# A later date for the first head's maxima, and half-tiles for the last four units' copies, in a fused attention and gated-MLP kernel

## The chip, the cores and the metric

The kernel runs on one core of one Trainium2 chip. The metric is the device time of one execution in microseconds (us). Before the change the median of three runs is 2565.24 us (2562.74 to 2565.86).

## The reference, cut to what matters

```python
def _A_ref(x, wqkv, wo):                      # 32 heads of 18
    q, k, v = split_heads(x @ wqkv)
    scores = jnp.einsum("bhqd,bhkd->bhqk", q, k) * (Dh ** -0.5)
    p = _softmax(scores, axis=-1)
    o = jnp.einsum("bhqk,bhkd->bhqd", p, v)
    return merge_heads(o) @ wo

def _B_ref(x, w_gate, w_up, w_down):
    g = jnp.einsum("bsd,df->bsf", x, w_gate)
    u = jnp.einsum("bsd,df->bsf", x, w_up)
    return jnp.einsum("bsf,fd->bsd", g * u, w_down)

xn = _layernorm(x)                            # x: 1 x 2048 x 576, F = 4608
out = x + _A_ref(xn, wqkv, wo) * _silu(_B_ref(xn, w_gate, w_up, w_down))
```

## The kernel before

Every product is made of float32r pieces: an operand is split into a high part and the rest, and three products of parts stand for one. The kernel has three stages: q, k and v from the normalised x (to about 190 us), a long middle (to about 2497 us), and the output products with `wo` (to the end).

**The middle.** TensorE is used as two halves of 64 rows, and two streams of matmuls run beside each other, stream 0 on rows 0 to 63 and stream 1 on rows 64 to 127. The gated MLP is cut into 72 units `u` = (chunk of 512 tokens, 256 columns of F). For a unit the streams make the up and gate products of its two blocks `n` = 2u and 2u+1 (27 matmuls of 512 columns for each block and stream, line 703), and after the gate and up products of the unit that follows they make the down products of unit `u` (48 matmuls of 288 columns for each stream, line 749). When the two of a block are done, VectorE multiplies them (line 715), ScalarE takes the high part into `hs[u]` (line 719), and GpSimd the rest (line 720). The down products of a half need the other half's rows too, so `turn_round` (line 726 and after) copies `hs[u]` with the halves exchanged into `hx[u]` by DMA. There is one buffer `hx`. For most units the copy is one pair of DMAs of 512 KB each, issued when the down products of the unit before are through (line 787). The last two units are copied in two parts, each as soon as its block of `hs` is there; of these, the first goes to a tile `hxl` in the buffer `acc` of the first accumulators, which are no longer used then.

**Attention** runs between these matmuls. Head by head, 64 products `a` (line 624) give scores whose row maxima VectorE takes (line 626); `max_rows` turns the 2048 maxima round and writes them into `pair`, rows 64 and after, with four DMAs from GpSimd's queue (line 646). Then 64 products `b` (line 656) give the transposed scores with the maximum subtracted, in two PSUM banks in turn, and ScalarE takes the exponential (line 658). The probabilities times v (line 667) take the whole array, in visits in which neither stream runs; the last visit of a head comes after its last exponential. After a head's last visit VectorE normalises (lines 679 to 684) and four DMAs store the result in `sot`; for the last head these are on SyncE's queue.

**The order** is not found on the chip: a planner (`order`, with `can_go`, `visit`, `b_ready` and their tables) runs while the program is built. It keeps a clock for each stream, free times for VectorE, ScalarE and GpSimd, and one clock for transfers (`moved`). From these it picks the next matmul. Every engine then works through its own list in that order and waits at semaphores. `rows_done[h]` is the planner's date for the maxima of head `h` in `pair`: the end of the last reduction plus `ROWS` = 6.0 us. `there["h", u]` is its date for the copy of `hs[u]`; a stream whose next matmul needs it later than its clock is held, and the other goes on alone. What the planner doesn't know is the time that an engine's queue needs to issue DMAs. After the last gate product `wo_load` (line 820 and after) loads `wo` with six DMAs from ScalarE's queue.

**After the middle** SyncE's queue loads the attention output back (`fetch_o`, lines 843 and 846), the silu of the MLP (line 871) and x (line 873), in the order of the code. ScalarE and VectorE split what came (lines 851 and 856), and 28 matmuls for each of 16 row tiles (line 1295) make the output.

Of the kernel before, what the change touches and what calls it, by code (L numbers as in the profile page):

```python
# [40 lines left out]
def kernel(  # L41
# [115 lines left out]
    units = [(c, q) for c in range(NCH) for q in range(NF2)]  # L157
# [160 lines left out]
    FIRST = (0, 1)  # L318
# [265 lines left out]
    n = 8  # L584
# [21 lines left out]
    with ExitStack() as mid:  # L606
# [103 lines left out]
        def gate_end(n, ps):  # L710
            u, j = divmod(n, 2)
            if j == 0:
                hs[u] = gp.tile([128, 2, 2, 512], FR, name="hs", bufs=2)
            h32 = us.pop(n)
            nc.vector.tensor_tensor(h32, ps, h32, op=OP.mult)  # L715
            if g_after(n):
                g_get(g_after(n))
            hj = hs[u][:, j]
            nc.scalar.activation(hj[:, 0, :], h32, AF.Copy)  # L719
            nc.gpsimd.tensor_tensor(hj[:, 1, :], h32, hj[:, 0, :].bitcast(FT), op=OP.subtract)  # L720
            if u == 0 or u >= len(units) - 2:
                turn_round(u, j)

        hx = {}

        def turn_round(u, j):

            if u >= len(units) - 2:
                if j == 0 and u == len(units) - 2:
                    hx[u] = accp.tile([128, 2, 2, 512], FR, name="hxl", tag="acc")  # L730
                elif j == 0:
                    hx[u] = gp.tile([128, 2, 2, 512], FR, name="hx", bufs=1)
                js = slice(j, j + 1)
            else:
                if u or j == 0:
                    hx[u] = gp.tile([128, 2, 2, 512], FR, name="hx", bufs=1)
                js = slice(0, 2) if u else slice(j, j + 1)
            for r in range(2):
                nc.sync.dma_start(hx[u][half[r], js].bitcast(FT), hs[u][half[1 - r], js].bitcast(FT))
# [28 lines left out]
        def down_end(r, u, s, ps):  # L768
            c, q = units[u]
            cs = slice(r * HALF, (r + 1) * HALF)  # L770
            if q == 0 and c >= 2:
                ready(sdone, 4 * c - 8 + s)
            a = sums(4 * c + s)[:, cs]
            if q == 0:
                nc.vector.tensor_copy(a, ps[:, 0:HALF])  # L775
            else:
                nc.vector.tensor_tensor(a, a, ps[:, 0:HALF], op=OP.add)  # L777
            if q == NF2 - 1 and c < NCH - 1:
                seen[c, s] = seen.get((c, s), 0) + 1
                if seen[c, s] == 2:  # L780
                    silu_store(4 * c + s)
            if s == 3:
                seen[u] = seen.get(u, 0) + 1
                if seen[u] == 2:
                    d_get(u + 1)
                    if u + 1 < len(units) - 2:
                        turn_round(u + 1, 1)

        def silu(t, new, end):
# [140 lines left out]
        TOTAL = H * N  # L930
        LEAD, MOST = 24, 40
        EARLY, LOAD, BEHIND = 0.17, 0.10, 10.0
        PACE, SKEW, PULL, FIRST, ROWS = 1.005, 3.0, 3.0, 2.0, 6.0
        slots, gone = [0, 0], [0.0, 0.0]
        clk, free = [0.0, 0.0], {"DVE": 0.0, "ACT": 0.0, "POOL": 0.0}
        TAIL = {"DVE": 0.095, "ACT": 0.115, "POOL": 0.04}
# [67 lines left out]
        def a_next(r=0):  # L1004
            nonlocal na
            h, i = divmod(na, N)
            feed(0, h, i)
            a_item(h, i, r)
            slot = turn["a"] % 2
            turn["a"] += 1  # L1010
            banks["a"][slot] = engine("DVE", issue(r, LONG), 0.60) + EARLY
            na += 1
            if i == N - 1:
                max_fold(h)
                max_rows(h)
                rows_done[h] = engine("DVE", 0.0, 0.85) + ROWS

        def b_ready(r=1):
            h = nb // N
# [137 lines left out]
        def order():  # L1157
# [6 lines left out]
            while any(heads) or na < TOTAL or nb < TOTAL or due:  # L1164
# [34 lines left out]
                if can and (at <= clk[r] + 0.01 and (goal <= clk[r] or blocked) or op is None and (at <= clk[r] or not held)):  # L1199
                    clk[r] = max(clk[r], at)  # L1200
                    score(r)
                elif op is not None:
                    length, first, work, end, (kind, n, k) = op
                    if first:
                        clk[r] = max(clk[r], next_free("g"))
                        slots[r] = banks["g"].index(next_free("g"))
                        banks["g"][slots[r]] = 1e9
                    work()
                    lands = issue(r, length)
                    gone[r] += length  # L1210
                    if end:
                        done = engine(end[0], lands, end[1])
                        banks["g"][slots[r]] = done + EARLY
                        if kind == "d":
                            if k == 47:
                                parts.setdefault(n, []).append(clk[r])
                                if len(parts[n]) == 2:
                                    downed[n] = moved(max(parts[n]) + 0.3, 1.18) if (n + 1) % NF2 and n + 2 < len(units) else 0.0
                                    if n + 3 < len(units):
                                        there["h", n + 1] = moved(max(parts[n]) + 1.0, 1.05)  # L1220
                        elif r == 0:
                            upped[n] = done
                        else:
                            gated[n] = done
                            fin = engine("ACT", done + 0.05, 0.535)
                            fin = engine("POOL", fin + 0.05, 1.29)
                            if n != 2:
                                anew = 4 * NF2 - UNSAVED <= g_after(n) < 4 * NF2
                                loaded[g_after(n) - 2] = moved(done - 0.4, 1.18) if (n // 2 + 1) % NF2 and not anew else 0.0
                            if n // 2 >= len(units) - 2:  # L1230
                                there["h", n // 2] = moved(fin, 0.524) - (0.0 if n // 2 < len(units) - 1 else 1.1)
                            elif n < 2:
                                there["h", 0] = moved(fin, 0.524)
                            for _ in range(2):
                                hot = n + 2 >= 2 * NF2 and n % (2 * NF2) in (34, 35, 0) and n + 2 < 2 * len(units)
                                for want in stacks:
                                    if hot and (want[0] is load_pair or n % (2 * NF2) == 2 * NF2 - 1):
                                        continue
                                    stacks.remove(want)
                                    send(want, fin + 1.4)  # L1240
                                    break
                    heads[r] = next(feeds[r], None)
                else:
                    clk[r] = max(clk[r] + 0.05, min(clk[1 - r] + 0.01, clk[r] + 0.3))
# [120 lines left out]
```

## Time and profile before

| | |
|---|---|
| median of three runs | 2565.24 us (2562.74 to 2565.86) |
| the profiled execution's own time | 2566.68 us |
| its span, first to last instruction | 2564.9 us |
| TensorE busy | 2544.2 us, 99% |
| VectorE, ScalarE, GpSimd busy | 75%, 57%, 24% |
| mean granted TensorE clock | 0.999 |
| chain that ended last | TensorE 95%, DMA 2%, VectorE 2% |

An engine's busy time is the union of its instructions; TensorE counts as busy when one of its two halves works, so 99% does not say that both do. A row of idle time names the instruction or transfer that ended it. Times in the rows are microseconds from the span's start.

### The profile page before, as it was taken

The page shows a single profiled execution, that of the slowest core. Times are in us where ns is not written, and L with a number is a line of the kernel's source. Part 1 is how long each engine was busy: PE and PEld are TensorE (multiplying, and loading weights), DVE is VectorE, ACT ScalarE, POOL GpSimd, SP SyncE. Part 2 cuts the span into 40 slices and gives each one's busy share as a digit, 9 for nine tenths or more (in the row PEclk, how much of TensorE's full clock was granted, in tenths as well). Part 3 has the DMA queues.
Part 4 walks back from the last instruction along what each step waited for, and adds up shares of the span by engine and source line. Part 5 has one row for each costly group of instructions (what it writes and reads, how often), then busy time and mean ns, then how long its engine had stood idle before and what let it go on. Part 6 is the DMA issues. An engine that isn't in the chain of part 4 may idle for free.

```text
span 2564.9 us, 59227 instructions
## 1 busy us (share of the span) xinstructions
PE 2544.2 (99%) x24360; PEld 2115.4 (82%) x24360; DVE 1933.2 (75%) x3377; ACT 1473.1 (57%) x2712; POOL 618.9 (24%) x687
## 2 busy tenths in 40 slices
PE   8999999999999999999999999999999999999998
PEld 7899888787888888878888888778888888888878
DVE  6208678877778888777878888777889887778537
ACT  5222666666666655556666665555656656556651
POOL 3214334443421111112311111111111121111125
PEclk9999999999999999999999999999999999999999
DMA  7796889889775656576766566565666666664567
GB/s 246 234 293 163 222 220 244 222 217 248 199 222 173 183 174 185 173 183 186 214 201 174 172 178 184 168 178 154 180 204 164 175 190 176 178 175 142 160 194 248
DMA packets 203979, 499.87 MB, mean 195 GB/s; under 512 B 57744, under 2 KB 125200, under 8 KB 165948
## 3 DMA queue, kind: packets, MB, share of 16 engines
q1 hardware_dynamic: 193020, 482.86, 66.7%
q0 software_dynamic: 9952, 11.74, 1.7%
q8 instruction: 192, 3.15, 0.5%
q10 hardware_dynamic: 736, 1.47, 0.2%
q14 instruction: 79, 0.65, 0.1%
HBM read 307.49 MB, written 107.61 MB: 162 GB/s over the span
## 4 chain that ended last, share of the span: by engine, by line
PE 95%; DMA 2%; DVE 2%; ACT 0%; SPq 0%; POOL 0%; issue 0%; ACTq 0%; DVEq 0%
PE pg L703 35%; PE pg L667 17%; PE pg L749 15%; PE pa L624 11%; PE pb L656 9%; PE pg L423 2%; PE pa L368 2%; PE pb L368 2%; PE pg L1295 1%; DVE mx L626 0%; DMA sqk<-hl 0%; PE pa L1295 0%; PE pb L1295 0%; DMA hx<-hs 0%; DMA xi<-in_A_x_dram 0%; DMA gin<-sg 0%
## 5 line engine op out<-in xcount | busy, mean ns | idle before, releaser
L626 DVE TENSOR_REDUCE mx<-pa 128x1 f32<-128x512 f32 x2048 | 1364.7, 686 | 222.7 <-PE pa L624 114.1
L658 ACT ACTIVATE pt<-pb 128x512 f32<-128x512 f32 x2048 | 1160.8, 598 | 532.9 <-PE pb L656 477.2
L703 PE MATMUL pg<-xc,wgu 64*128 64x512 f32 x7722 | 1358.1, 388 | 0.0
L703 PEld LDWEIGHTS pg<-xc,wgu 64*128 64x128 f32 x7722 | 1048.2, 184 | 36.0 <-DVE acc L775 0.2
L656 PE MATMUL pb<-pair,ring 64*128 64x512 f32 x2016 | 784.6, 395 | 2.6 <-DMA pair<-mt 2.6
L624 PE MATMUL pa<-pair,ring 64*128 64x512 f32 x2008 | 778.2, 393 | 1.1 <-DVE mx L626 1.1
L749 PE MATMUL pg<-wd,hs 64*128 64x288 f32 x3408 | 582.2, 292 | 0.3 <-DVE acc L777 0.2
L749 PE MATMUL pg<-wd,hx 64*128 64x288 f32 x3360 | 567.7, 292 | 0.0
L749 PEld LDWEIGHTS pg<-wd,hs 64*128 64x128 f32 x3408 | 489.0, 185 | 5.5 <-issue 0.8
L720 POOL TENSOR_TENSOR hs<-us,hs 128x512 fp32r<-128x512 f32 x144 | 186.3, 1293 | 1262.6 <-ACT hs L719 1251.5
L749 PEld LDWEIGHTS pg<-wd,hx 64*128 64x128 f32 x3360 | 477.9, 185 | 3.0
L667 PE MATMUL pg<-pt,vt 128*32 128x512 f32 x4096 | 454.8, 594 | 1.0 <-DVE acc L777 0.9
L624 PEld LDWEIGHTS pa<-pair,ring 64*128 64x128 f32 x2008 | 364.9, 184 | 68.3 <-issue 51.1
L656 PEld LDWEIGHTS pb<-pair,ring 64*128 64x128 f32 x2016 | 366.0, 184 | 9.5 <-issue 2.9
L667 PEld LDWEIGHTS pg<-pt,vt 128*32 128x32 f32 x4096 | 125.5, 110 | 284.7 <-issue 278.3
L777 DVE TENSOR_TENSOR acc<-acc,pg 128x288 f32<-128x288 f32 x544 | 231.6, 443 | 26.4 <-PE pg L749 22.7
L673 DVE TENSOR_TENSOR oc<-oc,pg 128x512 f32<-128x512 f32 x69 | 47.2, 685 | 217.3 <-PE pg L667 217.2
L719 ACT ACTIVATE hs<-us 128x512 fp32r<-128x512 f32 x144 | 91.0, 632 | 140.2 <-DVE us L715 139.2
L206 POOL TENSOR_TENSOR wgu<-wraw,wgu 128x384 fp32r<-128x384 f32 x129 | 129.5, 1020 | 98.3 <-ACT wgu L205 81.5
L671 ACT ACTIVATE oc<-pg 128x512 f32<-128x512 f32 x32 | 19.1, 598 | 188.3 <-PE pg L667 181.8
L646 POOL DMA_DIRECT2D pair<-mt x128 | 77.9, 614 | 178.5 <-DVE mt L641 171.9
L715 DVE TENSOR_TENSOR us<-pg,us 128x512 f32<-128x512 f32 x144 | 98.5, 684 | 26.3 <-PE pg L703 18.0
(147 smaller groups left out, 1394.4 us busy)
## 6 DMA issues: line engine op xcount, KB each, us to landing
wgu<-swg SPq DMA_DIRECT2D x94, 1152.0 KB
hx<-hs SPq DMA_DIRECT2D x138, 512.0 KB
wd<-swd SPq DMA_DIRECT2D x50, 1152.0 KB
swg<-wgu SPq DMA_DIRECT2D x36, 1152.0 KB
pair<-sqk SPq DMA_DIRECT2D x192, 144.0 KB
ring<-sqk SPq DMA_DIRECT2D x384, 72.0 KB
swd<-wd SPq DMA_DIRECT2D x18, 1152.0 KB
sqk<-hl SPq DMA_DIRECT2D x32, 512.0 KB
```

What stands on the lines that cost most here:

```text
L206: nc.gpsimd.tensor_tensor(w[:, 9 + b:12 + b, :], raw[:, b:b + 3, :], w[:, b:b + 3, :].bitcast(FT), op=OP.subtract)
L368: nc.tensor.matmul(p, wq[b, a], xcs[c][:, e, :], start=n == 0, stop=n == len(PAIRS) - 1)
L624: nc.tensor.matmul(p, q[rows, t * 128:(t + 1) * 128], k[rows, c * 512:(c + 1) * 512], start=True, stop=True)
L626: nc.vector.tensor_reduce(mx[h][:, t, c:c + 1], p, axis=AX.X, op=OP.max)
L656: nc.tensor.matmul(p, k[rows, t * 128:(t + 1) * 128], q[rows, c * 512:(c + 1) * 512], start=True, stop=True)
L658: nc.scalar.activation(pt[t, c], p, AF.Exp, scale=scale)
L667: nc.tensor.matmul(p[32 * c:32 * c + 32, :], vt[h // 2][:, t, 6 * (h % 2):6 * (h % 2) + 32], pt[t, c], start=t == ts[0], stop=t == ts[-1])
L703: nc.tensor.matmul(ps, gw[n][half[r], a, :], xg[i][half[r], e, :], start=k == 0, stop=k == len(TERMS) - 1)
L715: nc.vector.tensor_tensor(h32, ps, h32, op=OP.mult)
L720: nc.gpsimd.tensor_tensor(hj[:, 1, :], h32, hj[:, 0, :].bitcast(FT), op=OP.subtract)
L749: nc.tensor.matmul(ps[:, 0:HALF], (hx if k else hs)[u][half[r], j, a, s * 128:(s + 1) * 128], dw[u][half[r], k, j, e, :], start=n == 0, st ...
L777: nc.vector.tensor_tensor(a, a, ps[:, 0:HALF], op=OP.add)
```

## The change

Two things are changed. `CROWDED` = 9.0 takes the place of `ROWS` = 6.0 in the planner's date for the maxima of head 0. And the rule for the last two units (copy `hs` in two parts, each when its block is ready) now holds for the last four, 68 to 71; the even ones of them, 68 and 70, go into the buffer `acc`, the odd ones into `hx`. The planner's dates follow.

```diff
-            if u == 0 or u >= len(units) - 2:
+            if u == 0 or u >= APART:
                 turn_round(u, j)
 
         hx = {}
+        APART = len(units) - 4
 
         def turn_round(u, j):
 
-            if u >= len(units) - 2:
-                if j == 0 and u == len(units) - 2:
+            if u >= APART:
+                if j == 0 and u % 2 == 0:
                     hx[u] = accp.tile([128, 2, 2, 512], FR, name="hxl", tag="acc")
...
-                    if u + 1 < len(units) - 2:
+                    if u + 1 < APART:
                         turn_round(u + 1, 1)
...
-        PACE, SKEW, PULL, FIRST, ROWS = 1.005, 3.0, 3.0, 2.0, 6.0
+        PACE, SKEW, PULL, FIRST, ROWS, CROWDED = 1.005, 3.0, 3.0, 2.0, 6.0, 9.0
...
-                rows_done[h] = engine("DVE", 0.0, 0.85) + ROWS
+                rows_done[h] = engine("DVE", 0.0, 0.85) + (ROWS if h else CROWDED)
...
-                                    if n + 3 < len(units):
+                                    if n + 1 < APART:
                                         there["h", n + 1] = moved(max(parts[n]) + 1.0, 1.05)
...
-                            if n // 2 >= len(units) - 2:
+                            if n // 2 >= APART:
                                 there["h", n // 2] = moved(fin, 0.524) - (0.0 if n // 2 < len(units) - 1 else 1.1)
```

Most of the program stands as it did. On TensorE's list two stretches differ: 255 matmuls from the first `b` on, and 681 matmuls in the last 100 us of the middle. Lines after 722 are one higher in the changed kernel.

TensorE, where the products `b` of the first head begin (pb are their banks, line 656; pa are products `a` of the second head; pg with xc and wgu are up and gate products). Before:

```order
L749 MATMUL pg<-wd,hx 128x288
L656 MATMUL pb<-pair_1152,ring 128x512
L703 MATMUL pg<-xc,wgu 128x512
L656 MATMUL pb<-pair_1152,ring 128x512
L703 MATMUL pg<-xc,wgu 128x512 x2
L624 MATMUL pa<-pair_1153,ring 128x512
L703 MATMUL pg<-xc,wgu 128x512 x2
L624 MATMUL pa<-pair_1153,ring 128x512
L703 MATMUL pg<-xc,wgu 128x512 x9
```

In the changed kernel, the last rows ahead of its first `b` and those up to shortly after the second:

```order
L703 MATMUL pg<-xc,wgu 128x512 x15
L624 MATMUL pa<-pair_1153,ring 128x512
L703 MATMUL pg<-xc,wgu 128x512 x13
L624 MATMUL pa<-pair_1153,ring 128x512
L703 MATMUL pg<-xc,wgu 128x512 x4
L656 MATMUL pb<-pair_1152,ring 128x512
L703 MATMUL pg<-xc,wgu 128x512 x3
L656 MATMUL pb<-pair_1152,ring 128x512
L624 MATMUL pa<-pair_1153,ring 128x512
L703 MATMUL pg<-xc,wgu 128x512
L624 MATMUL pa<-pair_1153,ring 128x512
L703 MATMUL pg<-xc,wgu 128x512
```

Between the last down product and the first `b` there are now 57 matmuls of 512 columns, where there was none.

SyncE, from the copy for unit 67 on (hx and hxl from hs are the copies, wgu and wd the weights' loads, ring a load for attention). Before:

```order
L739 DMA hx<-hs 64x2048 x2
L197 DMA wgu<-swg 128x2304 x2
L265 DMA ring<-sqk 18x1024 x3
L240 DMA wd<-swd 128x2304
L739 DMA hx<-hs 64x2048 x2
L197 DMA wgu<-swg 128x2304 x2
L265 DMA ring<-sqk 18x1024 x3
L240 DMA wd<-swd 128x2304
L739 DMA hx<-hs 64x2048 x2
```

In the changed kernel:

```order
L740 DMA hx<-hs 64x2048 x2
L197 DMA wgu<-swg 128x2304
L740 DMA hxl<-hs 64x1024 x2
L197 DMA wgu<-swg 128x2304
L740 DMA hxl<-hs 64x1024 x2
L265 DMA ring<-sqk 18x1024 x3
L240 DMA wd<-swd 128x2304
L197 DMA wgu<-swg 128x2304
L740 DMA hx<-hs 64x1024 x2
L197 DMA wgu<-swg 128x2304
L740 DMA hx<-hs 64x1024 x2
L240 DMA wd<-swd 128x2304
```

The copies for units 68 and 69 now stand ahead of the load of `wd` that they stood behind.

ScalarE, at the end of the middle (pt from pb are the exponentials, us the end of an up product, hs the high part of a block of the last unit, wor the six loads of `wo`, and the names in brackets are the semaphores waited for, DMAHW those of transfers, of which there are eight). Before:

```order
L658 ACTIVATE pt<-pb 128x512 [waits PE_49] x6
L708 ACTIVATE us<-pg 128x512 [waits PE_49,Pool_49]
L658 ACTIVATE pt<-pb 128x512 [waits PE_49]
L719 ACTIVATE hs<-us 128x512 [waits DVE_49]
L825 DMA wor<-in_A_wo_dram 128x576 [waits DMAHW0_49,PE_49]
L825 DMA wor<-in_A_wo_dram 128x576 [waits DMAHW2_49]
L825 DMA wor<-in_A_wo_dram 128x576 [waits DMAHW3_49]
L825 DMA wor<-in_A_wo_dram 128x576 [waits DMAHW5_49]
L827 DMA wor<-in_A_wo_dram 64x576 [waits DMAHW6_49]
L827 DMA wor<-in_A_wo_dram 64x576 [waits DMAHW7_49]
L863 ACTIVATE wos<-wor 128x576 [waits DMAHW0_49,PE_49]
```

In the changed kernel:

```order
L708 ACTIVATE us<-pg 128x512 [waits PE_49,Pool_49]
L658 ACTIVATE pt<-pb 128x512 [waits PE_49] x3
L719 ACTIVATE hs<-us 128x512 [waits DVE_49]
L826 DMA wor<-in_A_wo_dram 128x576 [waits DMAHW3_49]
L826 DMA wor<-in_A_wo_dram 128x576 [waits DMAHW5_49]
L826 DMA wor<-in_A_wo_dram 128x576 [waits DMAHW6_49]
L826 DMA wor<-in_A_wo_dram 128x576 [waits DMAHW0_49]
L828 DMA wor<-in_A_wo_dram 64x576 [waits DMAHW1_49]
L828 DMA wor<-in_A_wo_dram 64x576 [waits DMAHW3_49]
L658 ACTIVATE pt<-pb 128x512 [waits PE_49] x13
L864 ACTIVATE wos<-wor 128x576
```

The last thirteen exponentials, which stood ahead of the loads of `wo`, now stand behind them, and the sixth load waits for the semaphore of the first.

## Rows read from the trace of the kernel before

**Rows 1.** The page, busy time of each engine (us, share of the span, instructions).
```profile
PE 2544.2 (99%) x24360; PEld 2115.4 (82%) x24360; DVE 1933.2 (75%) x3377; ACT 1473.1 (57%) x2712; POOL 618.9 (24%) x687
```

**Rows 2.** What TensorE's matmuls waited for: total us, times, longest.
```profile
PE pb L656 <- DMA pair<-mt: 2.6, 1, 2.6
```

**Rows 3.** Timeline at the first head: start, us, instruction [idle before it <- releaser].
```profile
255.98 1.28 ACT L658 ACT_TABLE_LOAD   x1
...
257.81 0.46 PE L656 MATMUL pb<-pair,ring 64*128 64x512 f32 x1 [2.63 <-DMA pair<-mt]
...
258.31 1.08 ACT L658 ACTIVATE pt<-pb 128x512 f32<-128x512 f32 x2 [1.05 <-PE pb L656]
```

**Rows 4.** TensorE by the microsecond: us, busy (matmuls), granted clock, DMA share, GB/s.
```profile
258.00:259.00 1.00, 1.00 (x9) 0.80 1.02 277
259.00:260.00 1.00, 1.00 (x8) 0.50 1.25 234
260.00:261.00 1.00, 1.00 (x8) 0.50 1.25 249
261.00:262.00 1.00, 1.00 (x7) 0.50 1.08 229
262.00:263.00 1.00, 1.00 (x12) 0.99 0.94 205
```

**Rows 5.** All matmuls in three stretches of the last 100 us of the middle.
```profile
2410.00:2415.00 5.00, 5.00 (x47) 1.00 1.00 135
2435.00:2440.00 5.00, 5.00 (x48) 1.00 1.03 295
2440.00:2445.00 5.00, 5.00 (x37) 1.00 0.98 289
```

**Rows 6.** Down products (line 749) alone, in two of these; weight loads stand second.
```profile
2410.00:2415.00 5.00, 1.90 (x12) 1.65 (x12) 1.00 1.00 135
...
2440.00:2445.00 5.00, 1.09 (x7) 1.04 (x8) 1.00 0.98 289
```

**Rows 7.** ScalarE's timeline where the middle ends (ACTq: issued by its queue).
```profile
2479.07 0.60 ACT L658 ACTIVATE pt<-pb 128x512 f32<-128x512 f32 x1
2480.48 0.63 ACT L719 ACTIVATE hs<-us 128x512 fp32r<-128x512 f32 x1 [0.81 <-DVE us L715]
2480.55 2.40 ACTq L825 DMA_DIRECT2D wor<-in_A_wo_dram  x4
2482.99 1.42 ACTq L827 DMA_DIRECT2D wor<-in_A_wo_dram  x2
2484.51 0.69 ACT L863 ACTIVATE wos<-wor 128x576 fp32r<-128x576 f32 x1 [3.40 <-DMA wor<-in_A_wo_dram]
...
2495.40 0.63 ACT L851 ACTIVATE hi<-o 128x512 fp32r<-128x512 f32 x1 [9.11 <-DMA o<-sot]
```

**Rows 8.** The last two loads of `wo`: duration ns min/median/max, first and last start.
```profile
L827 ACTq DMA_DIRECT2D wor<-in_A_wo_dram x2: 535/692/849, 2483.0 to 2483.6; - x2
```

**Rows 9.** TensorE's timeline: last visit, and the output products' begin and pause.
```profile
2480.90 3.64 PE L667 MATMUL pg<-pt,vt 128*32 128x512 f32 x32
...
2497.32 2.04 PE L1295 MATMUL pa<-wos,hi 128*128 128x288 f32 x12 [0.52 <-DVE acc L777]
...
2513.86 1.03 PE L1295 MATMUL pa<-wos,hi 128*128 128x288 f32 x6 [1.22 <-DVE ys L1304]
```

**Rows 10.** VectorE's timeline: the last head's first and last step after its last visit.
```profile
2484.69 0.69 DVE L673 TENSOR_TENSOR oc<-oc,pg 128x512 f32<-128x512 f32 x1 [3.88 <-PE pg L667]
...
2487.07 0.71 DVE L684 STREAM_TRANSPOSE oc<-tp 128x512 f32<-128x512 f32 x1
```

**Rows 11.** SyncE's queue after it: stores of the last head, reloads of heads.
```profile
2487.81 2.94 SPq L687 DMA_DIRECT2D sot<-oc  x4
2491.41 3.62 SPq L843 DMA_DIRECT2D o<-sot  x5
```

**Rows 12.** What SyncE's queue waited for, 2470 to 2520 us.
```profile
SPq L843 <- DMA hx<-hs: 0.5, 1, 0.5
```

## The prediction

> **What bounds the kernel now.** I read the page first: TensorE is busy 99% of the span, every other engine 75% or less [rows 1]. So only three things can move the time: TensorE waiting, TensorE at its lower clock, or one of its two halves working alone, which the busy time does not show. The list of what matmuls waited for has one DMA in it, once, for 2.6 us [rows 2]; the timeline puts it at 257.81 us, before the first product `b` of the first head, which waits for its maxima in `pair` [rows 3]. The windows by the microsecond show what came of it: once TensorE ran again, its granted clock was 0.80, 0.50, 0.50 and 0.50 of full speed for four microseconds, that is 1.2 instead of 2.4 GHz, and then full again [rows 4]. The third thing shows in the number of matmuls: 48 long ones in 5 us where both streams run, 47 and 37 in two stretches of the last 100 us, of which 12 and 7 are short [rows 5, 6]. Last I read the end of the middle engine by engine, because the output products there begin when a chain over four engines is through [rows 7 to 11].
>
> **The first head.** The maxima come when they come: four DMAs behind the second head's work, landed at 257.81. What the change moves is the matmuls. 57 long ones now stand before the first `b`. At 0.11 us each (5 us for 48, of which some four are cut by the stretch's edges) they take 6.4 us, so that `b` is reached at about 255.2 + 6.4 = 261.6, some 4 us after the landing. These 57 are up and gate products of unit 3 and products `a`; in the kernel before they followed directly on the first `b` without any wait of their own, so their operands were there by 258, and most were before. Removed: the wait, 2.63 us, and the lower clock, 0.20 + 0.50 + 0.50 + 0.50 + 0.01 = 1.71 us of full-speed work [rows 3, 4]. Sum 4.3 us.
>
> Added: ScalarE loads the table of the exponential just ahead of its first one. In the kernel before these 1.28 us lay inside the wait [rows 3]. Now an up product's end (its copy, 0.60 us) stands ahead of the load, and the third `b`, which needs the first one's bank, stands 18 matmuls (2.3 us, some of them alone in their half) behind the last matmul of that up product. The copy starts 0.45 us after that matmul (from `b` at 257.81 to its exponential at 258.31 it is 0.50 [rows 3]); then 0.60 + 1.28 + 0.60 follow, together 2.9 us. The third `b` waits 0.6 to 0.7 us. Bounds 0 (the load gets in before the copy) and 1.4 (load and gate's split both ahead). I take 0.7: the first head gives **3.6 us back** (2.9 to 4.3). A short wait like this I count without a clock penalty.
>
> The Trainium skill, "ScalarE: Activation LUTs", section "Table sets: the hidden batching unit", puts a table load at about 2.7 us. The trace has 1.28 [rows 3]. By the page another 1.4 us would be lost here, and the sum below would come to 2572.5 us.
>
> **The copies.** Those of units 68 and 69 leave earlier, and the planner no longer holds a stream for them. In the kernel before, 2440 to 2445 has 30 long and 7 short matmuls; a short one is 288/512 of a long one, so that is 34 of 48, and 2410 to 2415 is 35 + 6.7 = 42 of 48. The 14 and 6 that are missing, at 0.11 us, make 1.5 + 0.7 = **2.2 us** by which the last gate product comes earlier. The copies in parts cost SyncE four more issues; on that queue nothing near is late for it. The waits that the parts add are for buffers used two units before, long free; the first accumulators are through since chunk 2. I cost both at nothing; if a copy were late the down products behind it would wait, at up to 2 us.
>
> **What that sets free, and what is late next.** The planner now puts thirteen products `b` of the last head after the last gate product, where there were none. Their exponentials stand on ScalarE's queue behind the six loads of `wo`. The split that precedes the loads began at 2480.48 [rows 7]; 2.2 us earlier is 2478.3. The loads held the queue from 2480.55 to 2484.41, 3.86 us, and nothing else stood behind them but the split of `wo` itself. In the changed program the sixth also waits for the semaphore of the first, which had landed by 2484.51, 3.96 us after its issue [rows 7]; with 0.54 to 0.85 us for the sixth's own issue [rows 8] the queue is held 4.5 to 4.8 us. I take 4.7 (bounds 3.9 and 4.8). ScalarE is free at 2483.0.
>
> Thirteen exponentials at 0.60 us [rows 7] follow. The banks are two, so the last `b` goes in after the eleventh exponential, at 2489.6, and the last visit, 32 matmul rows in 3.64 us [rows 9], runs from 2489.9 to 2493.5. It had run from 2480.90 to 2484.54. So the last visit ends **9.0 us later**. TensorE is in order: the last unit's down products stand behind that visit, and the third of the thirteen `b` makes TensorE wait from about 2479.2 to 2483.6.
>
> Behind the visit comes the chain that I take as fixed: VectorE from 2484.69 to 2487.78, stores of the last head on SyncE's queue until 2490.75 [rows 10, 11], then the reloads of heads, which are behind these stores on the same queue though most of them don't need them. Of the 0.66 us to 2491.41, 0.5 was a wait for a copy of the last unit [rows 12] that will be long done. So the reloads are 8.5 us later, and with them ScalarE's split of the first (2495.40 [rows 7]) and the first output product (2497.32 [rows 9]): 2505.8.
>
> Two clock losses lie on this. The wait of 4.4 us is longer than the one of 2.63 us after which the clock fell [rows 3, 4]; but after it the exponentials set the pace, which hides most of the 1.7 us. I take 0.5 (0 to 1.7). Before the output products TensorE will have been idle from about 2500.5 to 2506, far longer than 2.63 us, and works at once at its own limit: 1.7 us more, as in rows 4 (0 to 3.4). Against that, the pause of 1.2 us at 2513.86 [rows 9] is taken up by TensorE being late anyway. The tail: 8.5 + 0.5 + 1.7 - 1.2 = **9.5 us more** (7 to 12).
>
> **The sum.** 9.5 - 3.6 = 5.9 us more. The profiled execution took 2566.68 us with a span of 2564.9, so it would take 2572.6; it lay 1.4 us above the median of the runs, so the median would go from 2565.24 to **2571.1 us**, +0.23%. The likeliest case's own range, from the bounds, is 2567.5 to 2574.5. A measurement of this kernel can tell about 0.2% (5.1 us) from no change, so the forecast stands near that line.
>
> **Rivals.** *The loads don't hold ScalarE* (not slower). The queue goes on to the exponentials while transfers are being set up. They would start at 2478.9, the eleventh ends at 2485.5, and the visit at 2489.4, 4.9 us late; reloads 4.4 late, clock and pause as above: tail +4.9, sum +1.3, 2566.5 us. It decides whether the first exponential behind the loads starts within a microsecond of the split. Against it: the split of `wo` began 0.1 us after the last issue, though that fits a wait for its data too [rows 7]. Chance 0.12. The Trainium skill, "DMA: Bandwidth & Descriptors", section "Anatomy of one DMA — SWDGE (gpsimd) path", gives about 50 ns for a sequencer's dispatch of a DMA, there on GpSimd's path. By that rule six would hold a queue for 0.3 us, and this rival would be the result; the trace has 3.86 us for six [rows 7].
>
> *The same mechanism, smaller*: the queue is held 3.9 us, the clock does not fall at the wait, the idle time before the output products costs less than 1 us. Tail 9.5 - 0.8 - 0.5 - 1.0 = 7.2, or less where the first head gives 4.3: sum +2.9, 2568.1 us, within 0.2%. Chance 0.30.
>
> *The first head's wait is exchanged, not removed*: the third and later `b`, held at the table load, or VectorE behind the products `a` that come sooner, stop TensorE for long enough that the clock falls again. Then only some 1 us is won there, and the sum is +8.5, 2573.7 us. For it speaks that the second head's `a` and the first `b` now lie closer; against it that VectorE idled right after the stall. Chance 0.10.
>
> *The tail is not late at all* (the planner's order holds on the chip, both gains arrive): -3.6 - 2.2 = -5.8, 2559.4 us. It would need exponentials that are not held, and stores that don't keep back the reloads. Chance 0.04.
>
> **How the numbers follow.** The forecast has the remaining 0.44. Slower by over 0.2%: 0.44 + 0.10 = 0.54. Within 0.2%: 0.30 + 0.12 = 0.42. Faster: 0.04. The range 2564.5 to 2575.5 takes in the first three rivals and the bounds, and leaves out the last one and the far ends of both sides.
>
> **What would show it.** Right: no matmul waits for `pair`, and no half clock near 260 us; an idle time of about 0.7 us before the third `b`; in the tail, the six loads on ScalarE's queue followed by thirteen exponentials in a row, TensorE waiting 3 to 5 us for the first of them, the last visit ending some 6 us later than before (9.0 less the first head's gain), the first output product some 5 us later, with a lower clock around it. Wrong: exponentials that run between the loads' issues; a matmul that waits for `hx` or `hxl`; or a new wait of microseconds between 258 and 270.

## The result, and the profile after

Over 19 runs each, the kernel before has a median of 2564.37 us (2561.18 to 2568.22) and the changed one of 2569.02 us (2564.31 to 2570.76): ratio 1.0018, 95% interval [1.0012, 1.0024]. It is 4.65 us slower, just inside the 0.2% within which the prediction calls a time the same; 5.9 us were forecast. The changed kernel's profiled execution took 2569.04 us, at its median, with a span of 2567.3 us. That of before lay 2.3 us above the median of its 19 runs, so the two spans differ by 2.4 us only. What follows counts between these two traces, and in medians where runs are compared.

The list of what TensorE's matmuls waited for, after (total us, times, longest), has no `pair` any more, and a new first entry from the middle:

```profile
PE pb L656 <- ACT pt L658: 4.5, 3, 3.8
```

**The first head**, timeline and TensorE's windows by the microsecond (us, busy, matmuls, granted clock, DMA share, GB/s), answering to [rows 3, 4]:

```profile
260.63 0.60 ACT L708 ACTIVATE us<-pg 128x512 f32<-128x512 f32 x1 [4.86 <-PE pg L703]
...
260.91 0.39 PE L656 MATMUL pb<-pair,ring 64*128 64x512 f32 x1
...
261.25 1.28 ACT L658 ACT_TABLE_LOAD   x1
...
263.20 0.49 PE L656 MATMUL pb<-pair,ring 64*128 64x512 f32 x1 [0.39 <-ACT pt L658]
```

```profile
260.00:261.00 1.00, 1.00 (x12) 1.00 0.94 213
261.00:262.00 1.00, 1.00 (x10) 1.00 1.14 229
262.00:263.00 1.00, 0.80 (x4) 1.00 0.96 221
```

The first `b` runs at 260.91 without a wait, the clock stays full, and what is left is 0.39 us before the third `b`, behind the copy of the up product and the table load.

**The end of the middle**, ScalarE (ACTq: issued by its queue), answering to [rows 7]:

```profile
2472.30 0.63 ACT L719 ACTIVATE hs<-us 128x512 fp32r<-128x512 f32 x1
2472.31 2.85 ACTq L826 DMA_DIRECT2D wor<-in_A_wo_dram  x4
2475.20 1.76 ACTq L828 DMA_DIRECT2D wor<-in_A_wo_dram  x2
2477.01 1.09 ACT L658 ACTIVATE pt<-pb 128x512 f32<-128x512 f32 x2 [4.07 <-DMA wor<-in_A_wo_dram]
...
2485.56 1.78 ACT L658 ACTIVATE pt<-pb 128x512 f32<-128x512 f32 x3 [0.16 <-PE pb L656]
```

The six loads hold the queue from 2472.31 to 2476.96, 4.65 us; the thirteen exponentials follow. TensorE, answering to [rows 9]:

```profile
2477.66 0.79 PE L656 MATMUL pb<-ring,pair 64*128 64x512 f32 x1 [3.82 <-ACT pt L658]
...
2486.64 3.64 PE L667 MATMUL pg<-pt,vt 128*32 128x512 f32 x32
...
2497.46 0.37 PE L1296 MATMUL pa<-wos,hi 128*128 128x288 f32 x1 [0.64 <-DVE acc L778]
2499.06 0.40 PE L1296 MATMUL pa<-wos,hi 128*128 128x288 f32 x1 [1.24 <-ACT hi L852]
2500.16 3.02 PE L1296 MATMUL pa<-wos,hi 128*128 128x288 f32 x10 [0.70 <-ACT hi L852]
```

TensorE waits 3.82 us for the first of these exponentials. The last visit ends at 2490.28 where it had ended at 2484.54. The first output product comes about when it did before, but the row of ten starts 2.8 us later than the first row of before, and slowly. The clock, in windows of 5 us:

```profile
2475.00:2480.00 5.00, 2.34 (x18) 0.62 1.02 276
2480.00:2485.00 5.00, 5.00 (x53) 0.70 0.40 85
...
2495.00:2500.00 5.00, 2.59 (x30) 1.00 0.78 220
2500.00:2505.00 5.00, 4.84 (x24) 0.66 1.01 316
```

It is at its lower level for some microseconds after both waits. Behind the visit, VectorE's first step and SyncE's queue (SPq), answering to [rows 10, 11]:

```profile
2490.42 0.69 DVE L673 TENSOR_TENSOR oc<-oc,pg 128x512 f32<-128x512 f32 x1 [4.23 <-PE pg L667]
```

```profile
2493.41 1.38 SPq L687 DMA_DIRECT2D sot<-oc  x4
2495.01 2.28 SPq L844 DMA_DIRECT2D o<-sot  x5
```

The starts of the same place in TensorE's list, us, put the pieces in order:

```
number of the matmul in the list       before     after   difference
1600   (ahead of the first head)       253.03    252.26    -0.77
2000   (behind it)                     298.63    294.06    -4.57
22960  (ahead of the last 100 us)     2402.35   2398.10    -4.25
24000  (among the output products)    2509.28   2513.30    +4.02
24359  (the last)                     2558.36   2560.92    +2.56
```

The first head gave 3.8 us and the end of the middle took 8.3. Among the output products, where the pause of 1.22 us in [rows 9] is gone, 1.46 came back. Between the two places where the order differs nothing of note happened.

### The profile page after: what moved, and what is told of

It reads as the page before. It is cut to its first block, busy times and chain, and to the rows that moved or that the text cites. A ratio compares the mean times of both kernels' runs of the same rounds, so it can differ in the third digit from the quotient of the medians.

```text
span 2567.3 us, 59234 instructions
## 1 busy us (share of the span) xinstructions
PE 2544.7 (99%) x24360; PEld 2114.7 (82%) x24360; DVE 1930.3 (75%) x3377; ACT 1472.1 (57%) x2712; POOL 617.3 (24%) x687
## 4 chain that ended last, share of the span: by engine, by line
PE 98%; DVE 1%; DMA 0%; ACT 0%; issue 0%; SPq 0%; ACTq 0%; DVEq 0%
PE pg L703 35%; PE pg L667 18%; PE pg L750 16%; PE pa L624 11%; PE pb L656 9%; PE pg L423 2%; PE pa L368 2%; PE pb L368 2%; PE pg L1296 1%; PE pa L1296 1%; DVE mx L626 1%; PE pb L1296 1%; DVE us L715 0%; DMA xin<-in_A_x_dram 0%; DMA wor<-in_A_wo_dram 0%; PE pg L354 0%
## 5 line engine op out<-in xcount | busy, mean ns | idle before, releaser
L750 PE MATMUL pg<-wd,hx 64*128 64x288 f32 x3312 | 559.6, 292 | 0.0
L750 PEld LDWEIGHTS pg<-wd,hx 64*128 64x128 f32 x3312 | 470.8, 185 | 2.8
```

What stands on the lines that cost most here:

```text
L750: nc.tensor.matmul(ps[:, 0:HALF], (hx if k else hs)[u][half[r], j, a, s * 128:(s + 1) * 128], dw[u][half[r], k, j, e, :], start=n == 0, st ...
```

## The experiments

All are timed against the kernel before, run beside them; the short diffs are against the changed kernel unless they say otherwise.

**One part at a time.**

```diff
-        APART = len(units) - 4
+        APART = len(units) - 2
```

> Only the later date for the first head's maxima; the copies in parts stay with the last two units. Theory (the two parts are independent; the loss is in the tail): the first head gives back 3.8 us, as in the changed kernel, and the tail is that of the kernel before: 2564.4 - 3.8 = 2560.6 us, ratio 0.9985. Rival (the wait is only passed on and comes back in the 2000 us that follow): within 1 us of the kernel before, ratio 0.9996 to 1.0004.

Measured: 2561.22 us against 2564.30, ratio 0.9989 [0.998, 0.9998]. 3.1 us faster, so the gain of the first head does not come back later, and this kernel beats both.

```diff
-                rows_done[h] = engine("DVE", 0.0, 0.85) + (ROWS if h else CROWDED)
+                rows_done[h] = engine("DVE", 0.0, 0.85) + ROWS
```

> Only the copies in parts for the last four units; the first head as before. Theory: the whole loss is here, 2569.0 + 3.8 = 2572.8 us, ratio 1.0033; the trace shows the wait for the maxima of 2.6 us and, in the last 100 us, the same wait of TensorE of about 3.8 us for an exponential behind the loads of wo. Rival (the loss comes from both changes together): below 2569, ratio under 1.0018.

Measured: 2571.81 us, ratio 1.0029 [1.0019, 1.004]: 7.5 us slower. Its list of waits has both:

```profile
PE pb L656 <- ACT pt L658: 3.9, 2, 3.7
PE pb L656 <- DMA pair<-mt: 2.4, 1, 2.4
```

7.5 - 3.1 = 4.4 us against the 4.65 of both together: the parts add up, and the whole loss lies in the copies' part. This trace holds a surprise too. TensorE waits 2.43 us at the first head, and the clock does not fall after it:

```profile
257.00:258.00 1.00, 0.29 (x2) 1.00 0.22 61
258.00:259.00 1.00, 1.00 (x12) 1.00 0.88 229
```

**What holds ScalarE.**

```diff
-                nc.scalar.dma_start(wov["raw"][:, k, :], wo[128 * k:128 * k + 128, :])
+                nc.sync.dma_start(wov["raw"][:, k, :], wo[128 * k:128 * k + 128, :])
...
-                nc.scalar.dma_start(wov["raw"][b:b + 64, 4, :], wo[512:576, :])
+                nc.sync.dma_start(wov["raw"][b:b + 64, 4, :], wo[512:576, :])
```

> The changed kernel with the six loads of wo on SyncE's queue, behind the copies for the last unit, so that nothing holds ScalarE between the last split and the thirteen exponentials; TensorE's order is the same to the row. Theory (the issue of six loads on ScalarE's queue is the cause): the wait of 3.8 us before the third of the thirteen products goes, and with it the half clock behind it; the last visit starts some 6 us earlier than 2486.6, the output products follow it, and a pause of 1.2 to 1.5 us returns among them: 2569.0 - 6.3 + 1.4 = 2564 us (2561 to 2566), ratio about 1.000. Rival (thirteen exponentials after the last gate product are too late by themselves, with two banks): the last visit moves by less than 2 us, 2567.5 us or more, ratio 1.0012 or more.

Measured: 2562.97 us, ratio 0.9994 [0.9985, 1.0003]; 6.05 us less than the changed kernel's median. ScalarE and the last visit in its trace:

```profile
2472.99 0.63 ACT L719 ACTIVATE hs<-us 128x512 fp32r<-128x512 f32 x1
2473.53 2.30 ACT L658 ACTIVATE pt<-pb 128x512 f32<-128x512 f32 x4
```

```profile
2480.86 3.64 PE L667 MATMUL pg<-pt,vt 128*32 128x512 f32 x32
```

TensorE's order is the same to the row. The exponentials now follow the split at once, and the visit starts 5.8 us earlier. The granted clock stays at 1.00 from 2470 to 2512 us, so the 6.05 us are those of the wait, of the late visit and of both stretches at the lower clock together. So the queue that issues the loads of `wo` was the cause. Of the pause that was expected back among the output products only 0.3 us came.

The control is the kernel before with the same edit:

> The kernel before with the six loads of wo on SyncE's queue: the control to the changed kernel with the same edit. Theory (the hold of ScalarE costs only where something that TensorE needs stands behind the loads, and before the change only the split of wo did): no change, ratio 0.9995 to 1.0005, where the same edit took 6 us from the changed kernel. Rival (the loads on ScalarE's queue cost time in both kernels): 3 us or more faster, ratio 0.9988 or less.

Measured: 2563.67 us against 2564.78, ratio 1.0000 [0.9991, 1.0009]. Where only the split of `wo` stands behind the loads, what the hold costs lies within some 2 us of nothing; the same edit took 6.05 us from the changed kernel.

The dose, twelve loads of half the rows on ScalarE's queue:

```diff
-                nc.scalar.dma_start(wov["raw"][:, k, :], wo[128 * k:128 * k + 128, :])
+                for p in (0, 64):
+                    nc.scalar.dma_start(wov["raw"][p:p + 64, k, :], wo[128 * k + p:128 * k + p + 64, :])
...
-                nc.scalar.dma_start(wov["raw"][b:b + 64, 4, :], wo[512:576, :])
+                for p in (0, 32):
+                    nc.scalar.dma_start(wov["raw"][b + p:b + p + 32, 4, :], wo[512 + p:544 + p, :])
```

> The changed kernel with the six loads of wo cut into twelve of half the rows, on the same queue of ScalarE: the same bytes, twice the issues. Theory (the number of issues sets how long ScalarE is held): it is held for some 8 to 9 us instead of 4.65, TensorE waits about 4 us longer, 2573 us, ratio 1.0034. Rival (what holds ScalarE is the bytes or the time to the landing): no change, 2569 us, ratio 1.0018.

Measured: 2574.11 us, ratio 1.0041 [1.0028, 1.0053], 5.1 us more than the changed kernel. Its queue and its wait:

```profile
2472.61 7.05 ACTq L827 DMA_DIRECT2D wor<-in_A_wo_dram  x8
2479.70 2.81 ACTq L830 DMA_DIRECT2D wor<-in_A_wo_dram  x4
```

```profile
2483.20 0.79 PE L656 MATMUL pb<-ring,pair 64*128 64x512 f32 x1 [9.06 <-ACT pt L658]
```

The same bytes in twice the issues hold the queue for 9.9 us instead of 4.65, so neither the bytes nor one landing sets the hold; it grows with the number of issues. The average of 0.8 us for each is made of unequal pieces, though. The six of the changed kernel (duration in ns, smallest, median and largest, then first and last start):

```profile
L826 ACTq DMA_DIRECT2D wor<-in_A_wo_dram x4: 389/444/1449, 2472.3 to 2473.7; - x4
L828 ACTq DMA_DIRECT2D wor<-in_A_wo_dram x2: 472/500/529, 2475.2 to 2476.5; - x2
```

The sixth load begins 1.3 us after the fifth, which took about 0.5: the 0.8 us between are its wait for the landing of the first, whose semaphore it uses again. With twelve, the last four wait likewise for about 1.1 of their 2.8 us.

**The wait, or the late visit?** TensorE's wait of 3.82 us looks like the loss itself. To tell it from the late visit, the planner is told of the hold, so that it puts other work into it:

```diff
                                     moved(max(clk), 1.47)
+                                    engine("ACT", max(clk), 4.5)
```

> The changed kernel; its planner books 4.5 us of ScalarE at the loads of wo. It then puts the thirteen products behind most of the down products of unit 70: no matmul should wait for an exponential behind the loads, but 138 instead of 93 down products stand ahead of the last visit and 51 instead of 96 behind it. Theory (what costs is how late the last visit is, and how little is left to cover the chain behind it): the visit moves from 2486.6 to about 2484, the idle time before the output products grows from about 3 to 6 us; 2567 us (2565.5 to 2568.5), ratio 1.001. Rival (what costs is TensorE's wait of 3.8 us and the half clock after it): both gone, 2563.7 us or less, ratio 0.9997 or less.

Measured: 2568.35 us, ratio 1.0014 [1.0006, 1.0023]. The long wait is gone from its list, and the visit is later still, where the theory had it earlier, at about 2484:

```profile
PE pa L1297 <- ACT hi L852: 3.6, 1, 3.6
PE pb L656 <- ACT pt L658: 1.1, 5, 0.4
```

```profile
2489.28 3.64 PE L667 MATMUL pg<-pt,vt 128*32 128x512 f32 x32
...
2501.05 2.02 PE L1297 MATMUL pa<-wos,hi 128*128 128x288 f32 x10 [3.60 <-ACT hi L852]
```

Without the wait the time is the same as with it within the intervals. TensorE's idle time has moved from ahead of the visit to ahead of the output products. But the lower clock, which the rival has going with the wait, is still there, so the run does not part the visit's place from the clock:

```profile
2480.00:2485.00 5.00, 4.41 (x19) 0.65 0.46 112
2485.00:2490.00 5.00, 5.00 (x48) 0.67 0.13 40
```

The thirteen products now stand nearly alone, each behind an exponential, 19 matmuls in 5 us; the longest wait is 0.4 us, and the granted clock falls there all the same. So it is shown that the wait can go without a gain. That what costs is the visit's place, because the output products wait for the chain behind it (VectorE, stores, reloads, splits), fits these rows and the table below, but no run shows it apart from the clock.

**The chain behind the visit.** On top of moving the loads, the four stores of the last head go to ScalarE's queue:

```diff
-                store(c, nc.gpsimd if h < H - 1 else nc.sync)
+                store(c, nc.gpsimd if h < H - 1 else nc.scalar)
```

> The changed kernel with the loads of wo on SyncE's queue and the four stores of the last head on ScalarE's, so that the reloads of the other heads no longer stand behind these stores. Theory (with the hold gone, what keeps the output products late is the chain from the last visit over VectorE, the stores and the reloads, under which only 96 down products are left as cover against 164 before the change): the products start about 2 to 3.5 us earlier than with the loads alone moved, 2560.5 us (2559 to 2563), ratio 0.9985. Rival (the order of the queue does not matter, since the first products need the last head as well): 2563 us, ratio 0.9995.

Measured: 2561.83 us, ratio 0.9987 [0.9978, 0.9996]; with the loads alone moved it was 0.9994 [0.9985, 1.0003]. The intervals overlap, so whether it helps stays open. In its trace, of an execution 1.6 us above the median, the reloads do run earlier, but the splits of `wo` on ScalarE now stand behind the stores' issue, and the products wait for those; then the clock falls:

```profile
2487.01 2.37 ACTq L687 DMA_DIRECT2D sot<-oc  x4
```

```profile
2495.29 2.05 PE L1296 MATMUL pa<-wos,hi 128*128 128x288 f32 x7 [1.41 <-POOL wos L865]
```

```profile
2495.00:2500.00 5.00, 4.71 (x19) 0.50 1.02 351
```

The clock does not fall in every execution of this kernel: of the eleven, the five whose mean granted clock is given as 1.000 took 2558.9 to 2561.8 us, the three with 0.998 took 2561.9 to 2563.4.

**Three units instead of four.**

```diff
-        APART = len(units) - 4
+        APART = len(units) - 3
```

> The changed kernel with the rule for the last three units instead of four: no product of the last head stands behind the last gate product, 159 down products follow the last visit. Theory (order of the last visit decides): the hold of ScalarE hurts nothing, and the copy of unit 69 in parts gives 1.5 us more than the first head's date alone: 2559.7 us, ratio 0.9982. Rival (a new wait: the last part of the copy for unit 71 now stands on SyncE's queue behind the stores of the last head, some 4 us late for the down products): 2562 to 2564 us, ratio 0.9992 to 1.0, with a matmul waiting for hx in the trace.

Measured: 2582.27 us, ratio 1.0067 [1.0055, 1.0079]. Both were wrong by far; the rival names one of two new waits, at less than half its size. TensorE's and SyncE's lists of waits:

```profile
PE pg L703 <- DMA wgu<-swg: 9.7, 1, 9.7
PE pg L750 <- DMA hx<-hs: 8.7, 1, 8.7
```

```profile
SPq L740 <- PE pg L750: 17.7, 1, 17.7
```

The second wait is the rival's: the last copy stands behind the stores of the last head on SyncE's queue. The first one is larger. With three, unit 69 is copied in parts into `hx` while unit 68's copy still stands in it; SyncE waits 17.7 us for the down products that read it, the load of the weights behind it is late, and TensorE stops for 9.7 us. So the number of units and the buffers belong together. With four, the copy of unit 68 lies in `acc`, and `hx` is free for unit 69 once unit 67 is through; with three, unit 68's own copy is still in `hx`.

**An earlier last head.** A shorter planned interval brings the last head forward, so that one product `b`, not thirteen, stands behind the last gate product:

```diff
-        PACE, SKEW, PULL, FIRST, ROWS, CROWDED = 1.005, 3.0, 3.0, 2.0, 6.0, 9.0
+        PACE, SKEW, PULL, FIRST, ROWS, CROWDED = 1.003, 3.0, 3.0, 2.0, 6.0, 9.0
```

> The changed kernel with a 0.2% shorter planned interval between products of the heads (PACE 1.003 for 1.005), which brings the last head some units forward: one product b instead of thirteen stands behind the last gate product, and 127 down products instead of 96 follow the last visit. Theory (place of the last visit and the cover behind it): the visit has to wait for one exponential behind the loads instead of thirteen, 2477.7 instead of 2486.6, the output products start at about 2491.5, and with the pause of 1.4 us back the time is 2561.5 us (2560 to 2564), ratio 0.999. Rival (the whole order is a new one, whose other waits eat the gain): 2565 us or more, ratio 1.0002 or more.

Measured: 2561.97 us, ratio 0.9991 [0.9982, 1.0001], with the loads still on ScalarE. The visit starts at 2477.52, as expected, and the row of products in earnest at 2494.42, some 3 us later than expected:

```profile
2477.52 4.15 PE L667 MATMUL pg<-pt,vt 128*32 128x512 f32 x32
...
2494.42 1.21 PE L1296 MATMUL pa<-wos,hi 128*128 128x288 f32 x7 [0.30 <-POOL wos L865]
```

With the loads moved as well:

> As the run with PACE 1.003, and the loads of wo on SyncE's queue. Theory: ScalarE is not held, so the last visit need not wait, the copies' 2.3 us arrive, and the time is the lowest of all, 2559.5 us (2558 to 2561.5), ratio 0.998. Rival (with the visit early the loads of the output stage set the end, and the pauses among the output products grow): no better than the run with PACE alone, 2561 us or more, ratio 0.9987 or more.

Measured: 2561.35 us, ratio 0.9988 [0.9979, 0.9996]. No better than the pace alone: the time is the rival's. Its reason is not in the trace, where the output products wait 1.1 us in all, 0.9 of it for VectorE. In this order only one exponential stood behind the loads.

One table sums up the end of the middle (us from the span's start; down products after the last visit are counted in the order):

```
kernel                         last visit   down products   output products   median,
                               starts       behind it       in earnest        ratio to before
first head's date alone        2476.77      164             2493.29           0.9989
pace 1.003                     2477.52      127             2494.42           0.9991
pace 1.003, loads on SyncE     2477.64      127             2492.83           0.9988
changed, loads on SyncE        2480.86       96             2495.26           0.9994
before                         2480.90      164             2497.32           1
changed                        2486.64       96             2500.16           1.0018
planner told                   2489.28       51             2501.05           1.0014
changed, twelve loads          2491.64       96             2504.88           1.0041
```

A later visit mostly goes with a longer time. It is not the visit's start alone: before, with 164 down products behind it, TensorE was idle for 0.52 us only ahead of the output products [rows 9], where the changed kernel, with 96, is idle for 2.58 us (0.64, 1.24 and 0.70) between the last down product and the row of ten. And the kernel whose planner was told has the later visit but not the longer time.

## Why the prediction was right, and where it was off

**Right in sign and cause; the size was 5.9 us, measured 4.65.** The likeliest case was the one that happened. By the prediction's own classes the time fell just on the other side of the line, within 0.2%, to which it gave 0.42 against 0.54. All marks of its case but one stand in the trace: no wait for `pair` and full clock at 260 us; a short wait before the third `b`; thirteen exponentials behind the six loads; a wait of TensorE "3 to 5 us" (3.82); the last visit "some 6 us later" (5.74); a lower clock around the output products. The one that does not is the first output product "some 5 us later": the first comes 0.14 us later, the row of ten 2.84. That the loads are the cause is shown by moving them, by their dose and by the control. The page's 50 ns for a dispatch on GpSimd's path in the Trainium skill, "DMA: Bandwidth & Descriptors", section "Anatomy of one DMA — SWDGE (gpsimd) path", does not carry over to ScalarE's queue here: the shortest of the six issues took 0.39 us. The likeliest case's own range, 2567.5 to 2574.5, should by its bounds (2.7 to 9.1 us more) have been 2567.9 to 2574.3; nothing hangs on it.

**The first head, forecast 3.6 us.** In the two traces it is 3.8: the wait and the lower clock gone as forecast, 0.39 us added where 0.7 was taken. In medians it is 3.1. The step that is too simple is the lower clock as a fixed part of the loss. The record allows a share to be put on it. Of three profiled executions with a wait of 2.4 to 2.6 us there (before, its control, the copies alone) the clock fell in two, and not in the third; without the fall only 2.0 us (2.43 less 0.39) are to be had. The record also has the mean granted clock of each execution. The fall alone takes 1.71 of some 2565 us, so an execution with it cannot be given as 1.000; both traces with it have 0.999. Of the 72 executions of the kernel before that were timed beside the experiments 16 have 1.000, with a median of 2562.8 us; the 52 with 0.999 have 2564.9. So in at least 16 of the 72 the clock did not fall. A term that is there in some executions should go in with a share.

**The copies, 2.2 us.** They arrive: in 2406 to 2411 and 2436 to 2441 of the changed kernel the streams make 34 + 23 x 0.56 = 47 and 28 + 33 x 0.56 = 46 long matmuls' worth of the 48 that five microseconds hold, where [rows 5, 6] came to 42 and 34. No copy is late. Their use is nil, as the prediction had it, since the last visit does not follow the last gate product.

**The hold, 4.7 us, and the visit, 9.0 us later.** Held 4.65 us, and the sixth load did wait for the landing of the first. Counted from the place ahead of the last 100 us (4.25 us earlier than before), the visit is 5.74 + 4.25 = 10.0 us later. That the 9.0 came so near is in part luck, for two errors cancel. The split ahead of the loads came 3.9 us earlier by this count (2480.48 less 2472.30, less 4.25), not 2.2; the thirteen products that no longer stand ahead of it, 1.4 us at 0.11 us each by estimate, were left out. And from the end of the hold to the visit it took 9.7 us (2476.96 to 2486.64), not 6.9: the lower clock after the wait was not hidden behind the exponentials, for which the prediction had set 0.5, and several of these waited 0.3 to 0.8 us for products.

**"The chain that I take as fixed" was the step that failed.** It was not fixed, because there were waits in it. The four stores took 2.94 us before and 1.38 us after. Before, most of the difference of 1.56 us is a wait of the second store for a copy of the last unit, which stands in the same list as the row of [rows 12]; the issues themselves were short (the three numbers are again smallest, median and largest, in ns):

```profile
SPq L687 <- DMA hx<-hs: 1.5, 1, 1.5
```

```profile
L687 SPq DMA_DIRECT2D sot<-oc x4: 292/303/415, 2487.8 to 2490.4; - x4
```

The prediction saw that this copy would be long done, but took out only the 0.5 us that the reloads waited for it. The five reloads took 3.62 us before and 2.28 us after, and that difference is one long issue:

```profile
L843 SPq DMA_DIRECT2D o<-sot x5: 343/430/1758, 2491.4 to 2494.6; - x5
```

```profile
L844 SPq DMA_DIRECT2D o<-sot x5: 342/419/430, 2495.0 to 2496.9; - x5
```

With the 0.44 us saved at the head of the reloads, these are 0.44 + 1.56 + 1.34 = 3.3 us. The row of ten is 2.84 + 4.25 = 7.1 us late where 8.5 were forecast (ScalarE's split of the first began 1.1 us behind them, at 2498.38, and not 0.4). The granted clock there lost the 1.7 us that were forecast, and the pause gave 1.46 for 1.2. By the table of places the whole tail is 6.8 us in place of 9.5. In medians the copies alone cost 7.5 us.

**The rivals.** "The loads don't hold ScalarE" is refuted. "The first head's wait is exchanged" too: 0.39 us stands there. "The same mechanism, smaller" came nearer in size (4.65 lies between its 2.9 and the forecast's 5.9), but its reasons were others: the clock did fall at both places, and it was SyncE's queue that no longer waited. That a kernel could gain both parts (2559.4 us) was not reached by any run: the lowest medians are 2561.2 to 2561.4.

**What stays open:** whether moving the stores helps at all; how much of the loss is the visit's place and how much the lower clock that came with it; and what ends the time in the kernel with an early last head and free queues, where the copies' 2 us ought to have come on top of the first head's 3.1 and did not.

## What to carry to other kernels

DMA issues are work for the engine whose queue makes them (here 0.39 to 1.45 us each on ScalarE's queue), and a planner that books only arithmetic will place urgent work behind them; put bulk loads on a queue where nothing urgent stands behind, or count the issues. A gain in the middle reaches the end only through the chain that starts the next stage: look which step starts that chain (here the last visit), how late it is, and how much independent work is left to cover it, and don't take a wait for the loss before a run has moved the wait. Before a stretch of a queue is taken as fixed, read all that it waits for, and ask of each wait whether the change removes it. When a transfer is allowed to leave earlier, look first at who still reads its buffer and at what stands behind it on its queue.

## What the runs showed that was not expected

A row of issues can hide a wait, and traffic alone does not make issues slow. With the first head's date alone the four stores took 1.38 us, as in the changed kernel, though the DMA engines were busy there (a share of 1.02) and nearly idle in the changed kernel (0.09 in 2490 to 2495 us):

```profile
2484.22 1.38 SPq L687 DMA_DIRECT2D sot<-oc  x4
```

```profile
2484.00:2486.00 2.00, 1.58 (x18) 1.00 1.02 223
```

Single issues do differ. Of the five reloads one took 1.76 us before, the others 0.34 to 0.43. Five of the six loads of `wo` took 0.39 to 0.53 us in the changed kernel, and one 1.45. What makes one issue long was not tried.

The lower clock is not a fixed follower of a wait. After 2.63 us and 2.52 us at the first head it fell to 0.50, after 2.43 us it stayed at 1.00. With the planner told, it fell with no wait of more than 0.4 us, while TensorE made 19 matmuls in 5 us. Before the output products, TensorE was busy 2.51 of 5 us with the loads on SyncE, and the clock stayed full; in the changed kernel it was busy 2.59 of 5 us, and it fell to 0.66 in the next window:

```profile
2490.00:2495.00 5.00, 2.51 (x23) 1.00 0.79 244
2495.00:2500.00 5.00, 4.74 (x35) 1.00 1.02 321
```

These two rows are of the kernel with the loads on SyncE; those of the changed kernel stand in the first section. What decides between the two was not tried.
